# All products in the 64-row tiling mode, with PSUM as four two-bank tiles: infini-attention and linear attention on one core

## Chip, cores, metric

One NeuronCore of a Trainium2 chip. The metric is the device time of one execution in microseconds. Where a version was run several times I quote the median and the range. Ratios are of fast runs alone; the medians hold two exceptions, named where they occur (one slow run of a_nowait, and five slow runs among 22 of the kernel before in one batch).

## The reference, cut to what matters

Four residual blocks on x (2048 tokens x 512, bf16), A, B, A, B, each on a layer norm. 32 heads of 16.

```python
# A: four segments of 512 tokens, causal softmax attention inside a segment,
#    plus a linear memory of the segments before
logits = einsum('bhqd,bhkd->bhqk', qs, ks) * scale + mask
a_dot  = einsum('bhqk,bhkd->bhqd', softmax(logits), vs)
a_mem  = (phi(qs) @ M) / (phi(qs) @ z + 1e-6)        # phi(t) = t + 1 if t > 0 else exp(t)
o      = g * a_mem + (1 - g) * a_dot                  # then o @ wo, added to x
# B: linear attention with softmax features
phi_q, phi_k = [softmax(pq), softmax(-pq)], [softmax(pk), softmax(-pk)]
o = (phi_q @ (phi_k^T v)) / (phi_q @ sum(phi_k) + 1e-6)
```

## The kernel before

TensorE makes the matrix products and writes them to PSUM, its accumulators; ScalarE (exps) and VectorE read them from there into SBUF, the working memory. Short names below: PV is softmax weights times values; M is A's linear memory and NM the product that reads it; KV, N and Zq are B's sums over keys, its numerators and its denominators; Wo is an output projection. A *tile* here is one buffer.

The program describes its work as a graph of operations on tiles; a list scheduler with a cost model orders them and gives each tile a buffer. It is run anew for every version, so a change of one buffer changes the order everywhere. What matters here:

```python
# PSUM: 8 banks as two two-bank tiles (scores, B's queries, N) and four one-bank tiles
dbl = [psum_tensor(f"D{i}", [128, 1024], F32) for i in range(2)]
sgl = [psum_tensor(f"G{i}", [128, 512], F32) for i in range(4)]
CAPG = {"gen": 3, "pv": 2, "nz": 1}       # at most so many of a kind alive in G

# a projection: 4 products over 128 rows into one bank
self.mm(lambda: [(ps.t[:, 0:512], xT.t[:, dt, tt*128:(tt+1)*128], W[:, dt, :], dt == 0, dt == 3)
                 for dt in range(4)], ...)

# a score tile: 8 heads x 128 queries; two products over 64 rows that run side by side,
# one into each bank. But for a few in the warm-up these are the only products of 64 rows.
self.mm(lambda: [(S.t[:, hf*512:(hf+1)*512], KT.t[64*hf:64*hf+64, j*128:(j+1)*128],
                  Q4.t[64*hf:64*hf+64, :, i*128:(i+1)*128], True, True) for hf in range(2)],
        ..., label="S", rows=64)
self.act(lambda: PT.t[:], lambda: S.t[:], ACT.Exp, 1024, [S], [PT], scale=0.25)
# ... then PV: 17-column products over 128 rows, one bank for two head groups
# ... (cut)
```

The softmax here doesn't subtract the row's maximum and nothing guards it: scores larger than these inputs give would overflow.

Of the kernel before, what the change touches and what calls it, by code (L numbers as in the profile page):

```python
# [9 lines left out]
ALU = mybir.AluOpType  # L10
# [5 lines left out]
D = 512  # L16
# [73 lines left out]
SWITCH = 100.0  # L90
# [3 lines left out]
class Graph:  # L94
# [39 lines left out]
    def op(self, ch, reads=(), writes=(), opens=(), kind="c", lat=None, label="", ndma=0, port=False, kb=0, rows=128):  # L134
        o = Op()
        o.id = len(self.ops)
        o.ch = ch
        o.deps = set()
        o.succ = []
        o.tiles = []  # L140
        o.opens = list(opens)
        o.kind = kind
        o.lat = lat
        o.label = label
        o.ndma = ndma
        o.need = False
        o.port = port
        o.kb = kb
        o.rows = rows
        o.vc = None  # L150
        for r in reads:
            self._touch(o, r, False)
        for w in writes:
            self._touch(o, w, True)
        o.deps.discard(o)
        self.ops.append(o)
        return o
# [65 lines left out]
    def forward(self, prio, pools, rule):  # L223
# [34 lines left out]
        rows = 128  # L258
# [37 lines left out]
        while len(order) < n:  # L296
# [25 lines left out]
            for e in ENGS:  # L322
# [39 lines left out]
                if e == "pe":  # L362
                    if o.rows != rows:
                        dur += SWITCH
                    rows = o.rows
# [11 lines left out]
                for s in o.succ:  # L377
                    left[s.id] -= 1
                    l2 = 0 if (e == "pe" and "pe" in s.ch and o.kind == "c") else lt
# [36 lines left out]
    def emit(self):  # L416
# [25 lines left out]
        for o in order:  # L442
# [17 lines left out]
            cand = [d for d in deps if not (d.kind == "c" and d.eng == "pe" and e == "pe") and not covers(kn, d)]  # L460
# [64 lines left out]
class Kernel:  # L525
# [20 lines left out]
    def mm(self, items, cols, reads, writes, opens=(), label="", rows=128):  # L546

        dur = sum(max(c / 2.4 + 2.5, 25.5) for c in cols)

        def fn(e):  # L550
            ins = None
            for out_ap, lhsT, rhs, st, sp in items():
                ins = e.matmul(out_ap, lhsT, rhs, start=st, stop=sp, tile_position=(basep(lhsT), basep(out_ap)))  # L553
            return ins
        return self.g.op({"pe": (dur, fn)}, reads, writes, opens, label=label, rows=rows)
# [22 lines left out]

    def tpe(self, out_ap, src, reads, writes, opens=(), label="", ev=None):

        ps = self.T(self.pG, "gen")
        pb = lambda: ps.t[:, :].bitcast(BF16)[:, 0:512]

        def fn(e):
            for k in range(4):
                ins = e.transpose(pb()[:, k * 128:(k + 1) * 128], src()[:, k * 128:(k + 1) * 128], self.ident[:])
            return ins
        self.g.op({"pe": (240.0, fn)}, list(reads) + [self.R("ident")], [ps], opens=opens, label=label + "p")
        if ev:
            self.evac(ev[0], lambda: ev[1](pb()), 512, [ps], writes, label=label + "e")  # L590
        else:
            self.evac(out_ap, lambda: pb().rearrange("p (a b) -> p a b", a=4), 512, [ps], writes, label=label + "e", fast=True)
# [11 lines left out]
    def alloc(self):  # L604
# [25 lines left out]
        self.Rz1 = sb("Rz1", [128, 8, 8, 2], BF16)  # L630
# [9 lines left out]
        self.pK = pool("pK", N_KT, [128, 512], BF16, {}, ("KT",))  # L640
        self.pV = pool("pV", 2, [128, 4, H, 17], BF16, {}, ("VT",))
        self.p1 = pool("p1", N_K1, [128, 512], BF16, CAP1, ("QT", "phiQ", "PhK", "phiKT", "E"))
        self.p2 = pool("p2", N_K2, [128, 1024], BF16, CAP2, ("ET", "EQ", "PT"))
        self.pT = pool("pT", N_VT, [128, 2, NG, 17, 8], BF16, {}, ("Vt",))
        self.pS = pool("pS", N_SM, [128, 256], F32)
        dbl = [self.es.enter_context(nc.psum_tensor(f"D{i}", [128, 1024], F32)) for i in range(2)]
        sgl = [self.es.enter_context(nc.psum_tensor(f"G{i}", [128, 512], F32)) for i in range(4)]
        self.pD = Pool("pD", dbl, psum=True)
        self.pG = Pool("pG", sgl, psum=True)
        self.pG.caps = CAPG  # L650
        self.pG.fifo = ("pv",)
        self.pools = [self.pK, self.pX, self.pQ, self.pV, self.p1, self.p2, self.pT, self.pS, self.pD, self.pG]
# [5 lines left out]
    def setup(self):  # L658
# [4 lines left out]
        def load(pairs, kb, writes, eng="sp", opens=()):  # L663
            dur = 780.0 if eng == "pool" else 470.0
            o = self.g.op({eng: (dur, lambda e: [e.dma_start(o, i) for o, i in pairs()])}, [], writes, opens, kind="d",
                          lat=1300.0 + kb / 0.25, label="load", ndma=1, kb=kb)
            self.loads.append(o)
            return o
# [22 lines left out]
        ldw(lambda: self.WA["o"], inp["A_wo"], R("WA", "o"))  # L691
# [6 lines left out]
        for g in range(NG):  # L698
            load(lambda g=g: [(self.WB["o"][:, g, :], inp["B_wo"][g * 128:(g + 1) * 128, :].rearrange("(h d) o -> d h o", d=16))],
                 128, [R("WBo", g)])  # L700
# [26 lines left out]
        v(lambda e: e.memset(self.eps8[:], 1e-6 / 128.0), 80, [], [R("eps8")])  # L727
# [31 lines left out]
        v(lambda e: e.tensor_copy(self.Rz1[:, :, :, 1], self.H8[:, None, :].to_broadcast([128, 8, 8])), 130,  # L759
          [R("H8")], [R("RzH")])  # L760

    def fold_weights(self):
# [12 lines left out]
        for k in ("k", "q"):  # L775
            raw = self.WBraw[k]
            W = self.T(self.pX, "raw")
            for dt in range(4):
              if FOLD_PE:
                self.tpe(lambda W=W, dt=dt: W.t[:, :, dt * 128:(dt + 1) * 128], lambda raw=raw, dt=dt: raw.t[:, dt, :], [raw], [W[dt]], [W], label="foldT")  # L780
              else:
                self.tr(lambda W=W, dt=dt: W.t[:, :, dt * 128:(dt + 1) * 128], lambda raw=raw, dt=dt: raw.t[:, dt, :], [raw], [W[dt]], label="foldT")
            for dt in range(4):
                ps = self.T(self.pG, "gen")
                self.mm(lambda ps=ps, dt=dt, W=W: [(ps.t[:, g * 128:(g + 1) * 128], W.t[:, g, dt * 128:(dt + 1) * 128],
                                                    Wbd.t[:, g * 128:(g + 1) * 128], True, True) for g in range(NG)],
                        [128] * 4, [W[dt], Wbd], [ps], label="fold")
                self.evac(lambda k=k, dt=dt: self.WB[k][:, dt, :], lambda ps=ps: ps.t[:, 0:512], 512, [ps], [R("WB", k, dt)], label="folde")
# [36 lines left out]
    def wproj(self, ps, col, W, wres, g, xT, opens=(), label=""):  # L825
        self.mm(lambda: [(ps.t[:, col:col + 512], W[:, dt, g * 128:(g + 1) * 128], xT.t[:, dt, :], dt == 0, dt == 3) for dt in range(4)],
                [512] * 4, [xT[i] for i in range(4)] + wres, [ps[col]], opens=opens, label=label)

    def vproj(self, ps, W, wres, tt, xT, opens=(), label=""):
        self.mm(lambda: [(ps.t[:, 0:512], xT.t[:, dt, tt * 128:(tt + 1) * 128], W[:, dt, :], dt == 0, dt == 3) for dt in range(4)],  # L830
                [512] * 4, [xT[tt]] + wres, [ps[0]], opens=opens, label=label)

    def phi(self, ps, dst, src=None):

        v = self.v
        e_ = self.T(self.p1, "phe")
        self.act(lambda: e_.t[:], lambda: ps.t[:, 0:512], ACT.Exp, 512, [ps[0]], [e_], label="phexp")
        v(lambda e: e.tensor_scalar(e_.t[:], e_.t[:], 1.0, None, op0=ALU.min), 202, [e_], [e_], label="phmin", port=True)
        if src is None:
            self.g.op({"dve": (602, lambda e: e.tensor_scalar(dst.t[:], ps.t[:, 0:512], 0.0, None, op0=ALU.max)),  # L840
                       "act": (478, lambda e: e.activation(dst.t[:], ps.t[:, 0:512], ACT.Relu))}, [ps[0]], [dst], label="phmax")
        else:
            v(lambda e: e.tensor_scalar(dst.t[:], src.t[:], 0.0, None, op0=ALU.max), 202, [src], [dst], label="phmax", port=True)
        v(lambda e: e.tensor_tensor(dst.t[:], dst.t[:], e_.t[:], ALU.add), 335, [dst, e_], [dst], label="phadd", port=True)  # L844


    def warm(self, ps):

        for k in range(N_WARM):
            def fn(e):  # L850
                for _ in range(2):
                    ins = e.matmul(ps.t[:, 0:512], self.onesb[:], self.onesb[:, None, :].to_broadcast([128, 4, 128]), start=True, stop=True)
                return ins
            self.g.op({"pe": (860.0 if k < 5 else 430.0, fn)}, [self.R("onesb")], [ps[0]], label="warm")
        ds = self.T(self.pD, "S")
        for n, m in ((512, 4), (17, 24), (128, 8), (512, 4)):
            def fn(e, n=n, m=m):
                for _ in range(m):
                    for r in (0, 64):
                        rhs = self.onesb[r:r + 64, None, :].to_broadcast([64, 4, 128]) if n == 512 else self.onesb[r:r + 64, 0:n]  # L860
                        ins = e.matmul(ds.t[:, r * 8:r * 8 + n], self.onesb[r:r + 64, :], rhs, start=True, stop=True, tile_position=(r, 0))
                return ins
            self.g.op({"pe": (m * max(n / 2.4, 25), fn)}, [self.R("onesb")], [ds], label="warm", rows=64)

    def qkproj(self, ps, k, raw, g, xT, opens, label):

        if raw:
            W = self.WAraw[k]
            self.mm(lambda: [(ps.t[:, 0:512], W.t[:, dt, g * 128:(g + 1) * 128], xT.t[:, dt, :], dt == 0, dt == 3) for dt in range(4)],
# [419 lines left out]
```

## Time and profile before

| | before |
|---|---|
| time, median of the first 3 runs | 556.56 us (555.61 to 558.91) |
| profiled span | 550.1 us |
| products, operations of ScalarE, of VectorE (profile) | 5632, 640, 965 |
| mean granted TensorE clock | 0.975 |

In all traces here the clock is granted either whole or by half; 0.975 of 550.1 us means 27 us at half. The busy times and stages are shown in the prediction. A busy TensorE in these profiles is not a TensorE at its peak, since a product is counted from its start to its modelled end (390 ns for one of 512 columns, while the next starts after 216): start-to-start times tell more.

### The profile page before, as it was taken

What the parts mean: (1) busy time and instruction counts of PE and PEld (TensorE: products, weight loads), DVE (VectorE), ACT (ScalarE), POOL (GpSimd) and SP (SyncE); (2) the same over time, 40 slices, a digit from 0 to 9 for tenths busy, and PEclk for the clock granted to TensorE, in tenths of its full rate; (3) what the DMA queues carried; (4) which work ended last, traced back from release to release, by engine and by line L of the source; (5) the groups of instructions that cost most, each with busy time, mean ns of one, the idle gap of its engine ahead of it and who ended that gap; (6) DMA issues with size and microseconds to landing.
All of it is one profiled execution on the core that took longest, in us unless ns stands there. A gap on an engine that the chain in (4) does not pass through costs nothing.

```text
span 550.1 us, 13819 instructions
## 1 busy us (share of the span) xinstructions
PE 503.2 (91%) x5632; PEld 255.7 (46%) x5632; DVE 439.2 (80%) x965; ACT 486.7 (88%) x640; POOL 226.3 (41%) x400
## 2 busy tenths in 40 slices
PE   7769798999999899998999799899999989999896
PEld 3223344444455454556644244344455444555552
DVE  5997998988686598778999598598886677876795
ACT  3967998999999989779998799999999999887984
POOL 5565654633753653300424354553274265330000
PEclk9978999999999899999999799899999999899999
DMA  6195333213111010000233332321111101100045
GB/s 191 55 265 76 69 69 74 54 42 57 36 35 41 11 40 20 21 2 2 49 78 78 86 74 53 60 40 30 54 36 39 40 22 30 30 12 1 11 127 151
DMA packets 90366, 31.07 MB, mean 56 GB/s; under 512 B 77472, under 2 KB 90304, under 8 KB 90304
## 3 DMA queue, kind: packets, MB, share of 16 engines
q1 hardware_dynamic: 90240, 30.17, 23.5%
q8 instruction: 44, 0.72, 0.5%
q14 instruction: 18, 0.15, 0.1%
q0 software_dynamic: 64, 0.02, 0.1%
HBM read 6.32 MB, written 2.10 MB: 15 GB/s over the span
## 4 chain that ended last, share of the span: by engine, by line
PE 49%; ACT 25%; DVE 15%; DMA 8%; issue 1%; POOL 1%; SPq 1%; ACTq 0%; POOLq 0%
PE G L553 34%; ACT p L559 22%; PE D L553 14%; DMA p<-p 5%; DMA pX<-p 2%; DVE p L568 2%; DVE p L1168 1%; DVE pQ L908 1%; DVE p L993 1%; DVE stats L794 1%; ACT p L812 1%; DVE pS L597 1%; DMA beta_sb<-in_A_beta_dram 1%; POOL p L973 1%; DVE p L844 1%
## 5 line engine op out<-in xcount | busy, mean ns | idle before, releaser
L559 ACT ACTIVATE p<-D 128x1024 bf16<-128x1024 f32 x384 | 378.3, 1053 | 30.9 <-PE D L553 28.4
L973 POOL TENSOR_SCALAR_AFFINE_SELECT p<-p 128x512 bf16<-128x512 bf16 x256 | 161.0, 654 | 181.2 <-ACT p L559 180.8
L553 PE MATMUL D<-pQ,pK 64*128 64x512 bf16 x640 | 118.9, 393 | 13.1 <-ACT p L559 10.8
L553 PEld LDWEIGHTS G<-pV,p 128*128 128x128 bf16 x2656 | 79.9, 96 | 38.2 <-issue 21.1
L553 PE MATMUL G<-pV,p 128*128 128x17 bf16 (+1 forms) x2656 | 90.8, 174 | 5.5 <-DMA p<-p 2.8
L559 ACT ACTIVATE p<-G 128x512 bf16<-128x512 f32 x112 | 69.5, 637 | 3.9 <-PE G L553 1.4
L553 PEld LDWEIGHTS D<-pQ,pK 64*128 64x128 bf16 x640 | 29.3, 93 | 82.8 <-ACT p L559 38.8
L1094 DVE TENSOR_REDUCE pS<-p 128x32 f32<-128x512 bf16 x64 | 42.8, 677 | 20.0 <-ACT p L559 19.9
L802 POOL TENSOR_SCALAR rstd<-mv 128x1 f32<-128x1 f32 x60 | 17.1, 287 | 80.0 <-DVE mv L795 79.9
L794 DVE BATCH_NORM_STATS2 stats<-X 128x6 f32<-128x512 bf16 x64 | 43.5, 691 | 2.6 <-DMA X<-in_A_x_dram 1.9
L1033 DVE TENSOR_TENSOR X<-X,G 128x512 bf16<-128x512 bf16 x48 | 32.7, 682 | 15.3 <-PE G L553 14.9
L1076 DVE TENSOR_TENSOR pT<-G,pT 128x1024 bf16<-128x1024 f32 x30 | 35.7, 1209 | 4.8 <-PE G L553 4.5
L553 PE MATMUL G<-WA_o,p 128*128 128x512 bf16 x128 | 33.8, 388 | 4.0 <-DMA p<-p 3.5
L553 PE MATMUL G<-WA_v,pX 128*128 128x512 bf16 x128 | 34.1, 395 | 3.8 <-ACT pV L567 1.9
L804 POOL TENSOR_TENSOR rstd<-rstd,mhalf 128x1 f32<-128x1 f32 x60 | 35.8, 598 | 3.7
L597 DVE RECIPROCAL pS<-G 128x32 f32<-128x32 f32 (+1 forms) x64 | 20.8, 327 | 19.4 <-PE G L553 18.9
L553 PE MATMUL G<-WB_o,p 128*128 128x512 bf16 x128 | 32.6, 380 | 2.2 <-DMA p<-p 1.8
L553 PE MATMUL G<-WB_k,pX 128*128 128x512 bf16 x128 | 32.5, 380 | 2.0 <-DMA pX<-p 1.3
L553 PE MATMUL G<-pX,WA_q 128*128 128x512 bf16 x112 | 30.8, 407 | 3.5 <-DMA pX<-p 2.6
L553 PE MATMUL G<-WB_v,pX 128*128 128x512 bf16 x128 | 33.4, 384 | 0.1
L553 PE MATMUL D<-pX,WB_q 128*128 128x512 bf16 x128 | 31.2, 379 | 0.0
L553 PE MATMUL G<-pX,WA_k 128*128 128x512 bf16 x112 | 29.6, 389 | 1.1 <-DVE p L993 0.6
(121 smaller groups left out, 689.8 us busy)
## 6 DMA issues: line engine op xcount, KB each, us to landing
pQ<-p SPq DMA_DIRECT2D x112, 32.0 KB, 1.8
out_dram<-X SPq DMA_DIRECT2D x16, 128.0 KB, 1.9
X<-in_A_x_dram SPq DMA_DIRECT2D x3, 512.0 KB, 4.1
pX<-in_B_wqkv_dram SPq DMA_DIRECT2D x3, 512.0 KB, 6.5
p<-p SPq DMA_TRANSPOSE x76, 2.4
pX<-p SPq DMA_TRANSPOSE x54, 2.4
X<-in_A_x_dram SPq DMA_DIRECT2D x4, 128.0 KB, 2.9
pX<-in_A_wk_dram SPq DMA_DIRECT2D x2, 256.0 KB, 4.3
```

The costliest lines, as they stand in the source:

```text
L553: ins = e.matmul(out_ap, lhsT, rhs, start=st, stop=sp, tile_position=(basep(lhsT), basep(out_ap)))
L559: return self.g.op({"act": (dur, lambda e: e.activation(out_ap(), in_ap(), func, scale=scale))}, reads, writes, opens, label=label)
L568: "dve": ((340 if fast else n / 0.96 + 65), lambda e: e.tensor_copy(out_ap(), in_ap()))}
L597: return e.reciprocal(o, i)
L794: v(lambda e: e.bn_stats(self.stats[:, t, :], self.X[:, t, :]), 602, [R("X", t)], [R("st", t)], label="bn")
L802: v(lambda e: e.tensor_scalar(rs, self.mv[:, t, 1:2], LN_EPS, None, op0=ALU.add), 170, [R("mv", t)], [R("rstd", t)], eng="pool", label="rstd")
L804: v(lambda e: e.tensor_tensor(rs, rs, self.mhalf[:], ALU.pow), 540, [R("rstd", t), R("mhalf")], [R("rstd", t)], eng="pool", label="rstd")
L812: "act": (590, lambda e: e.activation(xn.t[:], self.X[:, t, :], ACT.Identity, scale=rs, bias=nb))},
L973: v(lambda e, pt4=pt4: e.affine_select(pt4(), pt4(), [[0, 4], [1, 128]], ALU.is_ge, 0.0, base=0, channel_multiplier=-1), 560, [PT], [PT[hh ...
L1033: self.v(lambda e: e.tensor_tensor(self.X[:, t, :], self.X[:, t, :], ps.t[:, 0:512], ALU.add), 602, [R("X", t), ps[0]], [R("X", t)], label ...
L1076: v(lambda e: e.tensor_tensor(dst(), ps.t[:, None, 0:512].to_broadcast([128, 2, 512]).rearrange("p s (g d h) -> p s g d h", g=NG, h=8), rz ...
L1094: fn = lambda e, sgn=sgn, E=E, Z=Z: e.tensor_reduce(Z.t[:, sgn * 32:(sgn + 1) * 32], E.t[:, sgn * 512:(sgn + 1) * 512].rearrange("p (h d) ...
```

## The change

The intent: scores are the only products in 64 rows, so TensorE changes its tiling mode around every group of them, and each change costs about 100 ns (the prediction has the lines). If all products run on 64 rows there is no change left. A 128-row product is split into its two halves of the contraction. The two halves may not write one bank at the same time (the rule that the prediction takes from the Trainium skill; no run here tests it), so two products are made together in a two-bank tile: first the upper half of one and the lower half of the other, then swapped. So the second phase may not start before the first has ended, which takes a semaphore that TensorE waits for on itself.

```diff
-        dbl = [... psum_tensor(f"D{i}", [128, 1024], F32) for i in range(2)]
-        sgl = [... psum_tensor(f"G{i}", [128, 512], F32) for i in range(4)]
+        dbl = [... psum_tensor(f"D{i}", [128, 1024], F32) for i in range(4)]
+CAPD = {"S": 2, "gen": 2, "pv": 2, "nz": 1}

+    def proj(self, ps, ops, cols, reads, opens=(), label="", n=4):
+        def phases():
+            def item(b, h, k, ph):          # bank b, row half h
+                l, r = ops(b, h, k)
+                return ps.t[:, 512 * b:512 * b + cols], l, r, ph == 0 and k == 0, ph == 1 and k == n - 1
+            return [[(item(0, 0, k, 0), item(1, 1, k, 0)) for k in range(n)],
+                    [(item(1, 0, k, 1), item(0, 1, k, 1)) for k in range(n)]]
+        self.mm(phases, [[cols] * n] * 2, reads, [ps], opens=opens, label=label)

     # mm: one operation for each phase, each ordered after the one before by a semaphore
+            last = self.g.op({"pe": (dur, fn)}, reads, writes, ..., hard=(last,) if last else ())
     # emission: waits of TensorE on itself are left out, but not those
+            cand = [d for d in deps if (d in o.hard or not (d.eng == "pe" and e == "pe")) ...]

     # copies and exps now read both banks at once: 1024 columns instead of 512
-            self.evac(lambda: KT.t[:], lambda: ps.t[:, 0:512], 512, [ps[0]], [KT], label="Kev")
+            self.evac(lambda: KT.t[:], lambda: ps.t[:], 1024, [ps], [KT], label="Kev")
     # PV, KV, M, N, Zq, Wo, the transposes and the weight fold likewise (cut);
     # numbers of SBUF tiles and the split of B's keys are set anew (cut)
```

## The prediction

> **What bounds the kernel now.** I read the page's first part, then the table by stage (busy time of each engine in stretches), then the waits of ScalarE and TensorE, and last the timelines of those two, because busy time counts pipelined instructions at their full length.
>
> ```profile
> PE 503.2 (91%) x5632; PEld 255.7 (46%) x5632; DVE 439.2 (80%) x965; ACT 486.7 (88%) x640; POOL 226.3 (41%) x400
> L559 ACT ACTIVATE p<-D 128x1024 bf16<-128x1024 f32 x384 | 378.3, 1053 | 30.9 <-PE D L553 28.4
> L559 ACT ACTIVATE p<-G 128x512 bf16<-128x512 f32 x112 | 69.5, 637 | 3.9 <-PE G L553 1.4
> ```
>
> Two engines are close to full, TensorE and ScalarE, and ScalarE's idle time is almost all "waiting for TensorE's score tile" (28.4 us). By stage (columns: stretch, its length, then busy us of PE, PEld, DVE, ACT, POOL):
>
> ```profile
> 110.00:220.00 110.00, 106.60 (x1311) 53.94 (x1307) 85.48 (x172) 105.73 (x129) 51.46 (x90) 0.98 0.16 35
> 220.00:330.00 110.00, 101.11 (x1014) 54.85 (x1012) 91.31 (x227) 96.18 (x139) 33.82 (x65) 0.97 0.21 48
> 330.00:440.00 110.00, 104.29 (x1274) 50.58 (x1272) 85.50 (x178) 106.21 (x130) 51.58 (x91) 0.98 0.20 44
> 495.00:550.00 55.00, 47.65 (x460) 27.14 (x457) 39.04 (x91) 40.67 (x59) 0.79 (x2) 1.00 0.27 73
> ```
>
> In the attention stages (110 to 220, 330 to 440) ScalarE and TensorE are both over 95% busy. To see which has slack in truth I take start-to-start times. TensorE's timeline (start, length, then the group):
>
> ```profile
> 113.57 0.39 PE L553 MATMUL D<-pQ,pK 64*128 64x512 bf16 x2
> 113.89 1.04 PE L553 MATMUL G<-WB_k,pX 128*128 128x512 bf16 x4
> 114.86 0.39 PE L553 MATMUL D<-pQ,pK 64*128 64x512 bf16 x2
> 115.18 0.76 PE L553 MATMUL G<-pV,p 128*128 128x17 bf16 x24
> 115.88 0.39 PE L553 MATMUL D<-pQ,pK 64*128 64x512 bf16 x2
> ```
>
> A score pair (64 rows) takes 0.32 us to the next start, four projection products 0.97, 24 PV products 0.70. Inside runs of one kind the trace has 216 ns from one 512-column product to the next, 56 ns for 128 columns and 25 ns for 17, so the same pieces would take 0.22, 0.86 and 0.60. Each change between 128 and 64 rows therefore costs about 100 ns. I count 504 such changes in the trace: **50 us of TensorE**. The sum of all start-to-start floors without them is 423 us, with them 474, plus some 12 us for stretches at half the granted clock: TensorE has about 60 us of true slack in 550.
>
> ScalarE's timeline:
>
> ```profile
> 129.36 1.14 ACT L559 ACTIVATE p<-D 128x1024 bf16<-128x1024 f32 x1
> 130.27 0.73 ACT L559 ACTIVATE p<-G 128x512 bf16<-128x512 f32 x1
> 130.74 2.08 ACT L559 ACTIVATE p<-D 128x1024 bf16<-128x1024 f32 x2
> ```
>
> So 0.91 us for 1024 columns and 0.47 for 512: about n/1.2 ns + 50. Summed by that rule ScalarE needs 455 us in all; in 110 to 220 it needs 101 of 110, in 330 to 440 102 of 110, in 220 to 330 90 of 110, in 440 to 495 46 of 55. **Attention is bound by ScalarE, with TensorE right behind**; the query and key stages are bound by TensorE and by hand-overs; the first 55 us (ScalarE needs 31) and the last 20 are latency.
>
> **What the skill says.** "TensorEngine Tiling (Array Packing)", Key Properties: changing the tiling mode drains the array. The trace agrees: 312 and 319 ns where 216 are due. The same page, Gotcha 1: row tiles may not be in one PSUM bank together and software must order them; that is what the new semaphore is for, and no run here shows a violation. "TensorE: Matmul & The Clock Gate", Part 3: products on different row groups run concurrently, about 4 ns apart. Agrees: the warm-up already runs 48 products of 17 columns on 64 rows in 0.76 us, which is two every 25 ns, the pace of one 128-row product.
>
> ```profile
> 9.24 0.76 PE L861 MATMUL D<-onesb 64*128 64x17 bf16 x48
> ```
>
> "ScalarE: Activation LUTs", What ACT_TABLE_LOAD costs: 0.833 ns an element and successive ACTIVATEs overlap by about 93 ns; my 904 and 477 ns fit (0.834 ns an element, 50 ns fixed after overlap).
>
> **The change, part by part.**
> 1. Mode changes: 504 x 0.1 = **-50 us TensorE**. In 110 to 220 it is 15 us, in 330 to 440 14, in 220 to 330 4, after 495 none.
> 2. Splitting 128 rows into two halves in two banks: a pair takes the time of the product that it replaces, and the second phase swaps the halves, so projections, PV, KV, M and Wo are level (Wo: 8 pairs of 256 columns at 109 ns = 0.87 us against 4 x 216 = 0.86). Instructions roughly double.
> 3. Where half the product was zeros it shrinks: N, 256 x (56 - 29) = -6.9 us; transposes and pairs, 112 x 27 = -3.0; memory products (two groups of 8 and 128 columns before, now 48 x 112 ns), 10.2 - 5.4 = -4.8; fold -0.9. Together **-16 us TensorE**.
> 4. Semaphore between phases: 48 (K, Q, V) + 32 (B's keys and values) + 16 (queries) + 64 (Wo) + 6 (M) + 20 (KV) = 186 tiles with one wait each, and PV chains 64 tiles through four phases, 192 waits: 378. A bare wait costs about the pipeline's tail, 390 - 216 = 170 ns, plus the signal, say 230. The scheduler may put other products between the phases; I take a quarter as bare: 378 x 0.25 x 0.23 = **+22 us TensorE**, little of it where ScalarE binds. Net TensorE: -44 us.
> 5. ScalarE: 112 exps of 512 become 56 of 1024: 56 x 50 = -2.8 us; some 66 copies merge, -1.6; the 7 Relu reads vanish, -3.3. About **-8 us**, perhaps -5 more of copies that pass to VectorE.
> 6. VectorE: the K maximum reads bf16 from SBUF (17 x 0.6 becomes 12 x 0.34, -6), doubled minimum, add, reduction and copies save about 8, the memory product's normalisation (48 x 0.34 for 24 x 0.6), the uncopied values and the fp32 transposes give back 5: about **-10 us**.
> 7. PSUM: two two-bank and four one-bank tiles become four two-bank tiles that everything shares.
>
> On the path: attention (55 to 220 and 330 to 495) can give at most ScalarE's loss there (its 330 us hold 297 us of work, 33 us lost) plus about 9 of saved work. I expect a third of the loss and most of the saved work: **-17 us**. Queries and keys (220 to 330, 495 to 550): TensorE saves 8 of floors and 4 of switches and pays some 5 of waits, and the merged VectorE work helps: **-5 us**. Start: coarser K and Q tiles, more steps before the first score, fp32 transposes: **+2 us**. Sum -20: 556.6 - 20 = 537.
>
> **Rivals.**
> A. *PSUM becomes the bound.* Estimate for one attention segment of 40 score tiles: a score tile is held about 1.5 us (0.22 + 0.19 + 0.9 + 0.16), one per 0.9 us while scores run; PV tiles stay 5.5 us per 4.5 us of exps; a projection tile is held 2 x 0.86 + 0.2 + 1 to 2 us, some 57 us of tile time a segment of 45 us. Sum: 1.63 x 0.8 + 1.2 x 0.8 + 1.27 = 3.5 of 4 tiles. Before, the same demand was 1.3 of 2 and some 2.2 of 4. For it: 88% is tight, and a projection can now take the tile that a score needs. Against: the schedule is list-made with caps for each kind. It would eat the gain or more: 550 to 570, with ScalarE's wait for score tiles above 28 us.
> B. *TensorE really was the bound* through ordering: scores queue behind 0.9-us projections, so most of its 44 us come back as time. For it: ScalarE's waits are all for TensorE, and 96 us of ScalarE's span are lost in all. Against: in 110 to 220 only 9 us are lost. It gives 505 to 520.
> C. *The phase waits stand bare.* At 378 x 0.23 = 87 us TensorE would be above where it was: 565 or more. Against: scores of the next group are nearly always ready to go between.
>
> **Range and chances.** The central path gives 537. Rival B at full force gives 510, rival A 555 or so. 8 in 10: 514 to 557. A gain of over 2% means below 545.4. I give 0.63 to faster, 0.29 to the same, 0.08 to slower: the floors all fall, and only PSUM and the waits speak against it.
>
> **What would show it.** Right: no start-to-start times of 310 to 320 ns after 512-column products; TensorE busy clearly down (some 455 us) with about twice the products; ScalarE's busy share up to 90 to 93% of a shorter span; attention stages about 5% shorter, the last 55 us level. Step 4 is wrong if TensorE has many gaps of 150 to 250 ns ahead of second phases; step 7 if TensorE waits for ScalarE or VectorE (a tile to come free) more than the 26 waits and 12.8 us it now has for score tiles. The prediction as a whole is wrong if ScalarE's share falls, or if the time drops below 514, which would mean that TensorE's order, not ScalarE's work, set attention's pace.

## The result

The changed kernel takes 576.36 us (median of 4 runs, 571.37 to 579.57); the kernel before, in the same rounds, 557.73 us. Ratio 1.0329, 95% interval 1.0244 to 1.0415: **slower by 3.3%**. A ratio here is the mean time of one kernel's fast runs over that of the other's of the same rounds, so it is not quite the ratio of the medians. The prediction was wrong: it expected 537 us, a gain, and gave slower a chance of 0.08.

The page of the changed kernel, in the lines that answer to those shown of before (busy us and share of the span; then a group's busy time, mean ns of one, idle time ahead of it and what ended it):

```profile
PE 492.9 (85%) x10840; PEld 287.4 (50%) x10840; DVE 438.9 (76%) x848; ACT 472.6 (82%) x547; POOL 228.0 (39%) x398
PEclk9976998989989899997999998989996979999898
L560 ACT ACTIVATE p<-D 128x1024 bf16<-128x1024 f32 x440 | 421.2, 1032 | 71.3 <-PE D L553 65.5
```

Both engines that bounded the kernel have less work and a smaller share of the time. ScalarE now waits 65.5 us for TensorE's tiles where it waited 28.4. In the clock row (40 slices, tenths of full speed; 9 is 90% or more) 13 slices are below 9, where before there were 6:

```profile
PEclk9978999999999899999999799899999999899999
```

Half clock: 72.5 us against 27.3.

The drains are gone. TensorE's timeline of the changed kernel in attention (start, length, group, and in brackets the idle time before and what ended it):

```profile
153.29 0.39 PE L553 MATMUL D<-pQ,pK 64*128 64x512 bf16 x2
154.88 1.04 PE L553 MATMUL D<-WB_k,pX 64*128 64x512 bf16 x8 [1.21 <-ACT p L560]
155.75 0.40 PE L553 MATMUL D<-pQ,pK 64*128 64x512 bf16 x2
155.99 0.39 PE L553 MATMUL D<-WB_k,pX 64*128 64x512 bf16 x2
```

From the projection at 154.88 to the scores at 155.75 is 0.87 us, the bare four steps of 216 ns; from the scores to the next projection 0.24. But ahead of them TensorE stood idle for 1.21 us until ScalarE's exp freed a tile (by the program's order the projection takes the tile of a score whose exp ended at 154.74). That is the new picture. TensorE's waits (who waited for whom, us in total, times, longest), before:

```profile
PE D L553 <- ACT p L559: 12.8, 26, 0.8
PE G L553 <- DMA p<-p: 8.4, 12, 2.8
```

and after:

```profile
PE D L553 <- ACT p L560: 33.5, 66, 1.2
PE D L553 <- DMA p<-p: 6.7, 7, 2.0
PE D L553 <- DVE X L1049: 4.9, 10, 0.9
PE D L553 <- DVE p L1016: 4.1, 12, 0.8
```

This view counts only time in which no product is in flight. For a full account I matched the program's order of issue with the trace, product by product (5632 and 10840, the counts agree). For each group of products I took its start minus the end of the stream before it at full clock, less 100 ns at a change of mode, and gave gaps of over 15 ns to the wait that ended last: the last reader of the tile that held the PSUM buffer before ("tile"), TensorE's own first phase ("phase"), or data. Where that last reader had ended more than 0.25 us before, something else, often a DMA, really ended the wait; leaving these gaps out takes some 6 to 15 us off each total of tile waits, those below too (44 -> 102 becomes 34 -> 92), and the rise stays the same. The stages go from the first to the last score exp of a layer; "query" is from there to the next layer's first score exp or the end.

| stage | length us | work at full clock | drains | tile waits | phase waits | at half clock |
|---|---|---|---|---|---|---|
| start | 19 -> 20 | 13 -> 14 | 1 -> 0 | 1 -> 0 | 0 -> 1 | 0 -> 0 |
| attention 1 | 209 -> 210 | 153 -> 143 | 25.0 -> 0 | 22.7 -> 45.1 | 0 -> 7.8 | 13.7 -> 30.7 |
| query 1 | 57 -> 66 | 52 -> 52 | 0.2 -> 0 | 2.4 -> 6.5 | 0 -> 3.7 | 0 -> 6.8 |
| attention 2 | 206 -> 209 | 157 -> 151 | 24.3 -> 0 | 14.2 -> 42.0 | 0 -> 7.5 | 13.7 -> 27.3 |
| query 2 | 59 -> 73 | 49 -> 49 | 0.1 -> 0 | 4.5 -> 8.7 | 0 -> 4.9 | 0 -> 7.6 |
| all | 550 -> 578 | 423 -> 408 | 50 -> 0 | 44 -> 102 | 0 -> 25 | 27 -> 73 |

In attention the 49 us of drains that went came back as 50 us of waits for a tile and 15 us of waits for a phase, so its length hardly changed. In the query stages there were no drains to save, and they became 23 us longer, which is most of the loss. Which of the new waits does it, b_psum4 and a_nowait tell (below). The stage table of the profile for them (stretch, length, busy us of PE, PEld, DVE, ACT, POOL; then clock, DMA share and GB/s), before:

```profile
228.00:285.00 57.00, 54.25 (x570) 33.13 (x567) 48.26 (x120) 49.91 (x77) 9.55 (x20) 1.00 0.11 25
491.00:550.00 59.00, 51.65 (x510) 29.43 (x508) 41.16 (x93) 42.93 (x63) 2.01 (x4) 1.00 0.25 68
```

after:

```profile
230.00:296.00 66.00, 59.47 (x1230) 35.46 (x1223) 52.13 (x109) 48.94 (x69) 8.06 (x17) 0.95 0.10 21
505.00:578.00 73.00, 59.26 (x1256) 37.06 (x1252) 50.48 (x95) 44.22 (x61) 2.01 (x4) 0.95 0.27 58
```

ScalarE has the same work in them; it is spread over more time, and the clock is no longer whole.

### The profile page after: what moved, and what is told of

It reads as the page before. It is cut to its first block, busy times and chain, and to the rows that moved or that the text cites. A ratio compares the mean times of both kernels' runs of the same rounds, so it can differ in the third digit from the quotient of the medians.

```text
span 577.8 us, 24065 instructions
## 1 busy us (share of the span) xinstructions
PE 492.9 (85%) x10840; PEld 287.4 (50%) x10840; DVE 438.9 (76%) x848; ACT 472.6 (82%) x547; POOL 228.0 (39%) x398
## 4 chain that ended last, share of the span: by engine, by line
PE 52%; ACT 20%; DVE 18%; DMA 4%; issue 3%; SPq 1%; POOL 1%; ACTq 0%
PE D L553 51%; ACT p L560 19%; DMA p<-p 3%; DVE X L1049 2%; DVE p L1016 2%; PE D L870 1%; DVE stats L805 1%; DVE p L569 1%; DVE p L860 1%; DVE pV L569 1%; DVE pS L1090 1%; SPq L573 1%; DVE p L826 1%; DVE p L1177 1%; DVE pQ L922 1%
## 5 line engine op out<-in xcount | busy, mean ns | idle before, releaser
L560 ACT ACTIVATE p<-D 128x1024 bf16<-128x1024 f32 x440 | 421.2, 1032 | 71.3 <-PE D L553 65.5
L553 PE MATMUL D<-pV,p 64*128 64x17 bf16 (+1 forms) x5312 | 110.0, 171 | 6.3 <-issue 1.0
L553 PEld LDWEIGHTS D<-pV,p 64*128 64x128 bf16 x5312 | 96.1, 94 | 33.3 <-PE D L553 9.2
L1101 DVE TENSOR_TENSOR pT<-D,pT 128x1024 bf16<-128x1024 f32 x32 | 39.1, 1221 | 12.4 <-PE D L553 12.1
L1016 DVE TENSOR_TENSOR p<-D,pS 128x256 bf16<-128x256 f32 x112 | 46.0, 417 | 2.7
L553 PE MATMUL D<-WA_o,p 64*128 64x256 bf16 x512 | 43.3, 292 | 5.0 <-ACT p L560 2.3
L553 PE MATMUL D<-WB_o,p 64*128 64x256 bf16 x512 | 40.5, 286 | 7.8 <-DMA p<-p 5.7
L1090 DVE TENSOR_REDUCE pS<-p 128x64 f32<-128x1024 bf16 x32 | 38.3, 1211 | 7.4 <-ACT p L560 7.3
L553 PE MATMUL D<-WA_v,pX 64*128 64x512 bf16 x256 | 36.0, 408 | 3.1 <-DVE p L569 1.1
L553 PE MATMUL D<-WB_v,pX 64*128 64x512 bf16 x256 | 35.2, 396 | 3.0 <-DVE pT L606 1.4
L606 DVE RECIPROCAL pS<-D 128x32 f32<-128x32 f32 (+1 forms) x64 | 20.5, 323 | 21.2 <-PE D L553 20.9
L553 PEld LDWEIGHTS D<-WA_o,p 64*128 64x128 bf16 x512 | 24.3, 100 | 19.0 <-issue 8.6
```

Of the source, the lines that this page charges most:

```text
L553: ins = e.matmul(out_ap, lhsT, rhs, start=st, stop=sp, tile_position=(basep(lhsT), 0))
L560: return self.g.op({"act": (dur, lambda e: e.activation(out_ap(), in_ap(), func, scale=scale))}, reads, writes, opens, label=label)
L606: return e.reciprocal(o, i)
L1016: v(lambda e, pvv=pvv, rden=rden, part=part, dst=dst, k=k: e.tensor_tensor(part(dst), pvv()[:, :, k, :, 0:16], rden()[:, :, k, :, None].to ...
L1090: fn = lambda e, sgn=sgn, E=E, Z=Z: e.tensor_reduce(Z.t[:, sgn * 64:(sgn + 1) * 64], E[sgn].t[:].rearrange("p (h d) -> p h d", d=16), AX.X ...
L1101: v(lambda e, Vt=Vt, ps=ps, b=b: e.tensor_tensor(Vt.t[:, :, :, 0:16, :], ps.t[:, None, b * 512:b * 512 + 512].to_broadcast([128, 2, 512]). ...
```

## The experiments

**The theories.** *PSUM*: with all products in two-bank tiles, only four of them for everything, tiles come free too late; this is rival A of the prediction. *Waits*: the semaphore between the phases costs the time (rival C). *Clock*: a TensorE that idles more is granted half clock more often. *Order*: the drains were worth little in the first place because ScalarE sets the pace.

### b_psum4: the kernel before, only PSUM changed

```diff
-dbl = [... [128, 1024] ... range(2)];  sgl = [... [128, 512] ... range(4)]
+dbl = [... [128, 1024] ... range(4)];  self.pD = self.pG = Pool("pD", dbl, psum=True)
+self.pD.caps = {"S": 2, "gen": 3, "pv": 2, "nz": 1}
```

> The kernel before with nothing changed but PSUM: four two-bank tiles shared by all kinds of product instead of two two-bank and four one-bank tiles (at most 2 score, 3 general, 2 PV, 1 other tile alive); schedule made anew. Theory PSUM (too few tiles is what eats the gain): clearly slower than before, 580 us or more, with ScalarE's idle time ahead of score tiles up from 28 us to over 60 and the granted clock down. Theory waits (the semaphore between phases eats it): within 2% of before, 550 to 565, since there is no such wait here.

Measured: 604.82 us (600.63 to 607.7), ratio 1.0894 (1.0805 to 1.0982). ScalarE's wait for score tiles:

```profile
ACT p L559 <- PE D L553: 68.3, 81, 3.7
```

Tile waits of TensorE by the account above: 98 us, against 44; half clock 78.5 us. With no wait between phases and no product split, four shared tiles alone make the kernel 50 us slower. Theory PSUM holds; the waits are not needed to explain a loss. (The SBUF numbers were left as they were tuned for six tiles, so four tiles tuned for may cost less: see a_128.)

It also settles the query stages. Cut by the same marks they last 67 and 70 us here, in all 21 us more than before and about as much as in the changed kernel (66 and 73), with no phase waits and with only 3 us at half clock. So the tiles alone suffice for most of what the query stages lost (columns as in the stage table above):

```profile
250.00:317.00 67.00, 62.98 (x643) 37.59 (x639) 59.23 (x139) 51.92 (x81) 10.60 (x20) 1.00 0.10 22
532.00:602.00 70.00, 62.16 (x587) 34.92 (x583) 52.30 (x109) 47.89 (x72) 2.00 (x4) 0.98 0.24 57
```

### b_g3: one one-bank tile fewer

```diff
-sgl = [... range(4)]   CAPG = {"gen": 3, ...}
+sgl = [... range(3)]   CAPG = {"gen": 2, ...}    # and PhK no longer first-in-first-out
```

> The kernel before with one one-bank tile fewer (two two-bank and three one-bank tiles, at most 2 general ones; one first-in-first-out rule dropped so that it does not deadlock), nothing else changed. Theory PSUM: the number of tiles counts even where no kind shares with scores: 570 to 585, between before (555) and the version with four tiles (605). If sharing with the scores were what hurts, not the number: 553 to 562.

Measured: 577.56 us (574.14 to 579.14), ratio 1.0367 (1.027 to 1.0463). TensorE's tile waits rise to 71 us. One bank of eight (with its cap and that queueing rule) is worth some 20 us here, though no other kind of product shares with scores: the number of tiles counts by itself. ScalarE's waits for score tiles stay near those of before; the copies and the exps of B's keys wait instead:

```profile
ACT p L559 <- PE D L553: 32.9, 53, 3.3
ACT X L567 <- PE G L553: 9.0, 8, 1.7
ACT p L559 <- PE G L553: 7.4, 7, 2.9
ACT p L567 <- PE G L553: 6.2, 4, 3.4
```

### b_noswitch: the worth of the drains alone

```diff
-(S.t[:, hf*512:(hf+1)*512], KT.t[64*hf:64*hf+64, ...], Q4.t[64*hf:64*hf+64, :, ...])     # rows=64
+(S.t[:, hf*512:hf*512+256], KT.t[:, ...], Q4.t[:, 2*hf:2*hf+2, ...])                      # 128 rows
```

> Wrong result on purpose: the kernel before, but a score tile is made by two 128-row products of 256 columns (2 x 109 ns) instead of a 64-row pair of 512 (216 ns), so TensorE works as long and never changes mode (50 us of drains gone); half of each bank keeps old data. It gives the worth of the drains alone. My sum of the prediction (ScalarE binds attention, a third of its loss comes back): 8 to 17 us faster, 540 to 550. If TensorE's order were the true bound: 510 to 530. If ScalarE hides the drains wholly: 552 to 558.

Measured: 534.41 us (533.34 to 535.52), ratio 0.9627 (0.9576 to 0.9678), so 20.5 us faster than the 554.96 of the same rounds. (The comparison with the reference passes it although half of each score tile is old data, filled once at the start; why was not looked into, presumably A's part of the output is small against the tolerance. It is no version to use.) 50 us of drains are worth 20 us of time. TensorE's tile waits rose from 44 to 75 us: some 30 us of what the drains took turned into waiting for ScalarE to free the tiles, with PSUM as it was. TensorE's and ScalarE's waits for score tiles:

```profile
PE D L553 <- ACT p L559: 23.4, 57, 0.9
ACT p L559 <- PE D L553: 14.1, 25, 1.6
```

It missed its forecast of 540 to 550: a third of ScalarE's loss, 11 us, was too little, and the drains alone were worth about double. Neither "ScalarE hides them wholly" nor "TensorE's order is the bound" (510 to 530) holds.

### a_128: the changed kernel with 128 rows again

```diff
-return [[(item(0, 0, k, 0), item(1, 1, k, 0)) ...], [(item(1, 0, k, 1), item(0, 1, k, 1)) ...]]
+return [[(item(b, k),) for k in range(n)] for b in range(2)]      # all 128 rows, bank by bank
-hard=(last,) if last else ()
+hard=()                                                             # no wait between phases
# PV, KV, M, N, transposes, fold likewise; Zq in one bank
```

> The changed kernel in all but the tiling mode: products over 128 rows again, bank by bank, no semaphore between phases; the same four two-bank tiles, merged copies and merged exps; only scores in 64 rows, so the mode changes are back. Right result. Theory PSUM: slower than both, 585 us or more, since it has the few tiles and the drains; the 64-row mode itself then gains 10 us or more. Theory waits: about the time of before or faster, 545 to 560, since the waits are gone and the merged copies stay.

Measured: 581.45 us (578.84 to 582.46), ratio 1.0467 (1.0407 to 1.0527). Slower than both kernels (against the changed one the intervals just touch), by less than theory PSUM expected. The waits theory is refuted by its own forecast of 545 to 560. The four tiles with everything else of the change cost 26 us, half of what they cost in b_psum4: by this comparison the merged copies and the numbers of SBUF tiles, set for the new layout, give the other half back; which of the two was not tested.

### a_nowait and a_nowait_pv: the phase waits taken away

Each bank is fed by one row tile in both phases, so no order is needed and no bank is written from two row tiles; the sums are wrong on purpose. The order of issue is kept.

```diff
-[(item(1, 0, k, 1), item(0, 1, k, 1)) for k in range(n)]
+[(item(0, 0, k, 1), item(1, 1, k, 1)) for k in range(n)]
-(d in o.hard or not (d.eng == "pe" and e == "pe"))
+(not (d.eng == "pe" and e == "pe"))
```

> Wrong result on purpose: the changed kernel in exactly its own order, without the semaphore waits between phases (375 or so of them). Both phases of a bank are fed by the same row tile, so there is nothing to order; the mask fills with 1 so that no sum is zero. Theory waits: 545 us or less. Theory PSUM: 5 to 15 us faster than the changed kernel, 560 to 570, as the waits cost TensorE 36 us in the trace but ScalarE mostly waits for tiles; clock above 0.937 by 0.01 or so.

Measured: 568.22 us (565.16 to 574.29; the last is a slow run, the median of the three fast ones is 566.46), ratio 1.0217 (1.0144 to 1.0291); the profiled run's clock is 0.937, as with the waits. All the phase waits together are worth some 6 to 10 us (by the ratios 6, by the fast medians 10); the trace has 25 us of them, not the 36 of the expectation. Tile waits stay at 105 us. The query stages last 65 and 72 us where the changed kernel has 66 and 73: the phase waits are worth 2 us of the 23 there. The changed kernel without any of its phase waits is still slower than before. ScalarE's wait for score tiles hardly falls:

```profile
ACT p L560 <- PE D L553: 58.1, 61, 3.6
```

> Wrong result on purpose: the changed kernel in its own order, but only the 192 waits inside the PV chains are taken away (each bank fed by one row tile, mask filled with 1); the 186 of the other products stay. Taking all away gained 8 us. If the PV chains bear it: 568 to 571. If the projections' waits bear it: 574 to 577.

Measured: 573.18 us (571.38 to 574.25), ratio 1.0318 (1.0284 to 1.0353), against 1.0329 for the changed kernel in other rounds: no difference that can be told, and a time between the two forecasts. Phase waits halve (25 to 12 us in the trace). The waits of the PV chains, half of all, cost little; the gain of a_nowait belongs rather to the 186 waits of the other products, but the difference between the two runs (568 and 573) is no more than the spread within one of them, so I leave the split open.

### a_late12: PV later, in the changed kernel (a miss)

```diff
# scores and exps of both head groups first, then the PV products of both
-PTs + [PTs[i][0], PTs[i][1]] + [VT[j] ...]
+PTs + [PTs[i][0], PTs[i][1]] + PTg[1] + [VT[j] ...]
-CAP2 = {"PT": 10, ...}
+CAP2 = {"PT": 12, ...}
```

> The changed kernel, but the PV products of a pair of head groups start only when the exps of both groups are there, so that a PV tile is opened later and held shorter (5.2 us on average now); 12 instead of 10 probability tiles. Right result. Nothing changes in the tiling mode, the waits between phases or the number of instructions. Theory PSUM: 8 to 20 us faster than the changed kernel, 556 to 568, TensorE's waits for a tile to come free down from 102 us. Theory clock or waits alone: within 5 us of 576.

Measured: 587.99 us (586.55 to 593.6), ratio 1.0583 (1.0491 to 1.0676): slower, against the forecast. The part that I forecast did happen (a PV tile is held 4.5 us instead of 5.2, tile waits 102 to 83 us), but phase waits rose from 25 to 35 us, half clock from 72.5 to 96 us, and a wait of 7.2 us of ScalarE came in early in attention (at 36 us). By its exps the loss sits in the first query stage (73 us instead of 66) and the start (+3). So tile waits are not the whole account: a new order brings its own gaps. This holds for every version here but a_nowait and a_nowait_pv, which keep the order; single differences of some 10 us are to be read with that in mind. How much of the 12 us is the clock's I can't tell from this.

### a_dup: more work for TensorE

```diff
+# ahead of each score pair its first 256 columns, the same values: 109 ns each
+(S.t[:, b*512:b*512+256], KT.t[64*b:64*b+64, ...], Q4.t[64*b:64*b+64, 0:2, ...])
```

> The changed kernel, with 256 columns of each score pair calculated twice (the same values written again): 320 x 109 ns = 35 us more work for TensorE, about 1 us added to nothing else; right result. Theory clock (TensorE, idle more often, falls to half clock and loses 20 us or so by it): granted clock up from 0.937 to 0.955 or more and the time no longer, 565 to 578, in spite of 35 us more work. Theory PSUM without the clock: each score tile is held 0.1 us longer, 583 to 595.

Measured: 589.12 us (587.47 to 591.16), ratio 1.0587 (1.051 to 1.0663), clock 0.951, half clock 58 us. The clock part is as forecast in kind (busier, so less half clock), but the time grew by 13 us, inside the range of PSUM without the clock. So a better clock does not by itself win the time back. What the clock is worth is not isolated by this: 35 us of work cost 13 us of time while 14 us of half clock went away.

### b_late, v_nm, v_late_nm_pv3: tiles opened later, in the kernel before

```diff
# b_late: PV after the exps of both head groups, as in a_late12
# v_nm: the memory product starts only after that query tile's PV products
+pvops.append(<each PV op>)
+nmop.deps.update(pvops)
# v_late_nm_pv3: both, and
-CAPG = {"gen": 3, "pv": 2, "nz": 1}
+CAPG = {"gen": 3, "pv": 3, "nz": 1}
```

> The same delay of PV in the kernel before. PSUM is looser there (TensorE waits 44 us for tiles), so theory PSUM expects less: 2 to 8 us faster than before, 547 to 553. If it is faster, it is a version that beats both.

Measured: 552.48 us over 19 runs, ratio 0.9977 (0.995 to 1.0004): no gain that can be told. The PV tile is held 3.8 us instead of 5.0, but the memory product's tile 11.7 instead of 10.6, and tile waits are the same 45 us.

> The kernel before, but the memory product of a query tile (NM) starts only after that tile's PV products, so that its PSUM tile, which waits 10.6 us on average for the denominators now, is opened later. Right result. Theory PSUM: TensorE's waits for a tile fall below 44 us and the time falls by 3 to 10 us, 545 to 552. If it is not PSUM that counts: 553 to 558.

Measured: 551.46 us (549.32 to 553.91), ratio 0.9922 (0.9892 to 0.9953): 0.8% faster, little but clear of noise. The memory product's tile is held 1.7 us instead of 10.6; tile waits fall from 44 to 38 us.

> The kernel before with both delays (PV after the exps of both head groups, NM after PV) and up to three PV tiles alive. Right result. Theory PSUM: the best of the versions, 5 to 12 us faster than before, 543 to 550, which would beat both kernels; if it is not PSUM that counts, 552 to 558.

Measured: **540.88 us** (539.75 to 542.65), ratio 0.9741 (0.9713 to 0.9769), right result: it beats both kernels, by 14.5 us and some 35 us. Its page and ScalarE's first wait:

```profile
PE 500.8 (93%) x5632; PEld 257.1 (48%) x5632; DVE 443.1 (82%) x979; ACT 480.2 (89%) x626; POOL 224.0 (41%) x400
ACT p L559 <- PE D L553: 27.7, 45, 3.3
```

The drains are all there (490 changes of mode); TensorE's tile waits are 35 us and half clock 23.9 us, the least of all versions. The one-bank tiles are in use 2.25 of 4 on average, against 2.76. Without any change to a product, PSUM buffers held shorter, with three PV tiles allowed, gained most of what removing all drains gained (20 us), and more than the 5 to 12 forecast. The third PV tile was not tried alone, and the two delays alone gave nothing (b_late) and 4 us (v_nm), so how the 14.5 us divide is open.

## Why the prediction was wrong, point by point

- **Step 1** (drains, -50 us of TensorE): right in size: of 504 changes of mode none is left.
- **Steps 2 and 3** (split products keep their pace, some shrink by 16 us): right. The work at full clock fell from 423 to 408 us.
- **Step 4** (378 waits, a quarter bare, 22 us of TensorE): right in size: 129 of them (a third) cost over 15 ns, 24.6 us together, 190 ns each. They are worth some 6 to 10 us of time.
- **Step 5** (ScalarE -8, perhaps -13): ScalarE's busy time fell by 14 us. **Step 6** (VectorE -10): its busy time stayed at 439 us, since it took over copies (6 us more of them) and does 112 reads of 256 columns (46.0 us) where it did 64 of 256 and 24 of 512 (42.8 us).
- **The step that failed is 7 and what the path sum made of it.** "Four two-bank tiles that everything shares" got no term of its own in the sum; it stood only in rival A. I expected attention to change by -17 us, queries and keys by -5, the start by +2. Measured: +4, +23, +1. The saved TensorE time in attention met tile waits that grew by 50 us; in the query stages there was nothing to save, and new losses had little cover, because TensorE's work at full clock already filled 52 of 57 us and 49 of 59 there. The trace has tile waits (+8), phase waits (+9) and 14 us more at half clock (7 us at most) in them; b_psum4, with the four tiles alone, has the same length. By the prediction's own sign step 7 is wrong: TensorE's waits for ScalarE to free such a tile went from 26 (12.8 us) to 66 (33.5 us). And ScalarE's busy share fell from 88% to 82% where 90 to 93% was expected.
- **Rival A had the mechanism**: "a projection can now take the tile that a score needs", and ScalarE's wait for score tiles is 65.5 us, over the 28 that it named. Its size was too small: 550 to 570 with the gain already inside; four tiles and the rest of the change make 581 with the drains still in (a_128), or 605 in the old structure. My estimate was 3.5 of 4 tiles in use; the trace has 3.20 on average, with all four in use 44% of the time. (Of before I estimated 1.3 of 2 and 2.2 of 4; that trace has 1.37 and 2.76, with all four one-bank tiles in use 27% of the time and both others 51%, so PSUM was already tight, which could have been read before the change.) I read 88% as "tight" where it means that a new group of products often finds none free; and I weighed it against "caps for each kind", which say who waits, not whether.
- **Rivals B and C** are refuted as explanations of the result: removing the drains alone gave 20 us, not 40 or more; removing the waits alone left the kernel slower than before.
- **Readings that were a little off**: TensorE is 94.8% busy in 330 to 440 us, not over 95%. Of what the prediction takes from "ScalarE: Activation LUTs" the slope fits; the overlap of successive exps is 103 ns or more in the trace (median 129).
- **What I left out**: the clock. I took the loss at half clock as a constant 12 us. It follows how much of the time TensorE's array streams (last section). The work issued at half clock, which takes twice its time, was 12 us before and 35 us after, so by this estimate TensorE lost some 23 us more. What that costs in time is not settled: in the four runs of the changed kernel the slowest three had clocks of 0.937 to 0.940 (575.67 to 579.57 us) and the fastest 0.954 (571.37 us), which is a correlation only, and a_dup did not isolate it.

In one chain, each from chip runs, against before: four tiles with merged copies, 128 rows, 1.047 (a_128); with 64 rows and no drains or waits, 1.022 (a_nowait); with the waits, 1.033. The new mode did gain 2.5% without its waits and some 1.4% with them; it was given its tiles at a price of 4.7%.

One number was to be had before any run and was overlooked. The program prints its scheduler's own length at each build; that model knows tiles, drains and phase waits, but always runs at full clock. As ratios to before (526.9 us) it gives b_psum4 1.086, b_g3 1.045, a_128 1.044, b_noswitch 0.970, near the measured 1.089, 1.037, 1.047 and 0.963. For the changed kernel it gives 531.5 us, 1.009: no gain, since in it the tiles already eat all that the mode saves. The rest of the measured 1.033, some 2.4%, it does not explain, nor a_dup (1.032 against 1.059) and a_late12 (0.995 against 1.058); the clock is a suspect, not shown.

## What to carry to other kernels

Before a mode that needs two accumulators at once, count the accumulator buffers that each product holds and for how long, from first write to last read, and look at how often none is free; an engine that gets faster only fills the buffers sooner. Saved time of one engine counts only where its next wait is not for a buffer that a busier engine frees: 50 us of drains were worth 20 even with all of PSUM as it was. And the cheap direction comes first: opening accumulators later (after their other inputs are there), with one more of a kind allowed, cost no instruction and gained 2.6%.

## What the Trainium skill lacked or had wrong

- "TensorE: Matmul & The Clock Gate" ties the fall to half clock to idle windows and gaps of over some 3 us in its table of states and its rules; its section on "psum-queue depth-cycling" says that frequent micro-idles do it too, but not how many. In these traces no idle window is needed: over 13 profiles, time was cut into windows of 3.41 us on the grid of the clock's changes, and the share taken that the array would stream at full clock (columns x rows / 128). Of 1941 windows at full clock, all 131 with a share up to 0.36 were followed by half clock, and none with more than 0.39 was; 144 falls in all. So here a window in which the array streams for 0.36 of the time or less, be it for waits or for small products, is followed by a slow one.
- "TensorEngine Tiling (Array Packing)" says that a change of mode drains the array but not what it costs: some 95 to 107 ns here after products of 512 columns (310 to 323 ns from start to start where 216 are due).
- The same page says that row tiling raises PSUM pressure, without a size. Here two-bank tiles for everything raised TensorE's waits for a free tile from 44 to 102 us (and from 44 to 98 in b_psum4, with no row tiling at all but for scores), and one bank fewer of eight cost some 20 us.
- No page gives the price of ordering two row tiles by a semaphore as one figure: 190 ns for each wait that stood bare (24.6 us in 129 waits); the other two thirds of the waits cost under 15 ns each.
